# Attention on one Trainium2 core: squares on GpSimd between VectorE passes that read PSUM, two masked evacuations of Q, and more zero matmuls

## The chip, the cores and the metric

The kernel runs on one core of a Trainium2 chip. A core has a matmul engine (TensorE, "PE" in the profile), a vector engine (VectorE, "DVE"), an activation engine (ScalarE, "ACT"), a general engine (GpSimd, "POOL"), which in these kernels works on SBUF alone, and a queue engine (SyncE, "SP"). They run side by side, each takes its own instructions in order, and they wait for each other on semaphores. SBUF and PSUM are the on-chip memories; these kernels use PSUM as eight banks, each for a 128x512 tile of fp32.

The metric is the device time of one execution in microseconds (us), as the median of several runs. Each run also has a mean *granted clock* of TensorE: 1.0 is full speed, 0.5 is half. A run on one core is called slow when it is more than 1.5% above the fastest of the same kernel. Verdicts use the other runs ("fast" ones).

## The reference

Multi-head attention, with batch 1, 2048 positions, width 448 and 16 heads of 28:

```python
qkv = (x @ wqkv).reshape(B, S, 3, H, Dh).transpose(2, 0, 3, 1, 4)
q, k, v = qkv[0], qkv[1], qkv[2]
scores = jnp.einsum("bhqd,bhkd->bhqk", q, k) * (Dh ** -0.5)
p = softmax(scores, axis=-1)
o = jnp.einsum("bhqk,bhkd->bhqd", p, v)
return o.transpose(0, 2, 1, 3).reshape(B, S, D) @ wo
```

There are 16 x 2048 x 2048 exponentials. In tiles of 128 keys by 512 queries that is 1024 tiles, and they set the time of this kernel.

## The kernel before

The work is cut into 16 *windows*: four groups of four heads, times four blocks of 512 queries. A window has 16 rows (128 keys each), and a row has four tiles, one for each head. For each tile TensorE computes scores into PSUM. Another engine turns them into probabilities in SBUF. When all four tiles of a row are there, TensorE adds the row's weighted sum to the output bank `PO`.

Two routes make the probabilities:

- ScalarE takes two tiles at a time (128x1024) with one exponential instruction. It has two double banks, `PA`.
- *Side tiles* go to VectorE. The scores are scaled so that their integer part is the exponent of a bf16 number. The low 16 bits of the fp32 word hold the fraction, and a cubic polynomial of this fraction corrects the mantissa. Three banks, `PD`, serve the side tiles, and also every projection of Q, K, V and the output.

The order of all instructions is made by a small simulation inside the kernel. It walks through time with assumed durations, and decides for each tile which route it takes. On the chip the order is fixed. If an instruction takes longer than assumed, everything behind it on its engine is late. The side route of the kernel before, cut:

```python
def start_pair(tiles, t):                       # two side tiles at once
    for k, (n, sop, slot) in enumerate(tiles):  # pass 1: reads PSUM, writes f16
        p1s.append(add(Op("DVE", 0.6, lambda: nc.vector.tensor_scalar(
            out=DU[b][:, k*QW:(k+1)*QW], in0=lo, scalar1=1.0/65536, scalar2=SS-0.5, ...), ...)))
    q  = add(Op("DVE", ..., nc.vector.tensor_tensor(out=DQ[b], in0=DU[b], in1=DU[b], op=mult)))   # 128x1024
    v  = add(Op("DVE", ..., nc.vector.tensor_scalar(out=DV[b], in0=DU[b], scalar1=C3, scalar2=CE)))
    gq = add(Op("DVE", ..., nc.vector.tensor_tensor(out=DG[b], in0=DQ[b], in1=DV[b], op=mult)))   # 128x1024
    for k, (n, sop, slot) in enumerate(tiles):  # last pass: PSUM plus the cubic
        f = add(Op("DVE", 0.6, nc.vector.scalar_tensor_tensor(out=PTD[..], in0=PD[..], scalar=.., in1=DG[b][..])))
...
if ... d_inflight[0] < ND and backlog(t) < DBACK:      # may one more side tile start?
    ...
    pend_pair.append((n, op, s))
    if len(pend_pair) == 2:                            # only in pairs
        start_pair(list(pend_pair), t); pend_pair.clear()
...
# nothing else to do and little done in the last 3.4 us: one zero matmul,
# but not before the first row of a window
if activity(t) < BAR and ...:
    if pv_next[0] == 0 or j > 0:
        nc.tensor.matmul(out=PO[:], lhsT=zeros[:], rhs=zrow[:], start=first, stop=first, ...)
```

GpSimd does one thing in the steady state: at each window's end it multiplies the copied output by the reciprocal row sums (`OT <- OSB, RRB`, 15 times).

## Time and profile before

| | before |
|---|---|
| median of the first runs | 457.5 us (454.8 to 459.3) |
| span of the profiled run | 450.8 us, mean clock 0.966 |
| ScalarE busy | 417.8 us (93%) |
| VectorE busy | 394.7 us (88%) |
| TensorE busy | 386.6 us (86%) |
| GpSimd busy | 23.0 us (5%) |
| exponential instructions of 128x1024 | 440 |
| side tiles | 144 |
| zero matmuls | 76 |

The page of the kernel before, parts 1 and 2. Part 1 has the busy time and share of each engine. In part 2 each digit is one fortieth of the span, in tenths of busy time. PEclk is the granted clock in tenths.

```profile
span 450.8 us, 7221 instructions
...
PE 386.6 (86%) x2664; PEld 126.2 (28%) x2664; DVE 394.7 (88%) x702; ACT 417.8 (93%) x453; POOL 23.0 (5%) x33
...
PE   7898888889989879789988888879898888888894
...
DVE  4689989889969999999969999999999999489922
ACT  2599999899999999999999999999999999989991
...
PEclk9999999699999998999999999999999989969998
```

ScalarE is at 9 nearly everywhere, and VectorE is close. The clock shows a 6 in two slices. The busy share alone doesn't say what ScalarE loses. For that one looks at the spacing of the exponentials in the timeline. They start 0.905 us apart when nothing is missing. 439 x 0.905 = 397 us, but from the first to the last start it is 416 us. Part of the missing time is seen as waits of the exponentials (line L740) for their scores (waited for: us in total, times; the first exponential of all is 3.4 us of it):

```profile
  PE PA_177 L504: 6.8, 9
  PE PA_178 L504: 4.4, 7
```

Windows of 5 us in the kernel before. The columns are the busy time of PE, weight loads, DVE, ACT and POOL, then granted clock, DMA share and GB/s:

```profile
core 0: us, PE busy (x) PEld busy (x) DVE busy (x) ACT busy (x) POOL busy (x), PEclk, DMA share, GB/s
70.00:75.00 5.00, 4.92 (x36) 1.57 (x36) 4.75 (x9) 5.00 (x7) 0.00 (x0) 1.00 0.00 0
75.00:80.00 5.00, 3.45 (x26) 0.82 (x23) 4.93 (x10) 5.00 (x6) 0.00 (x0) 1.00 0.02 4
80.00:85.00 5.00, 4.42 (x20) 0.94 (x20) 4.93 (x10) 4.37 (x6) 0.00 (x0) 0.69 0.05 8
85.00:90.00 5.00, 4.99 (x23) 0.82 (x22) 3.74 (x6) 3.85 (x4) 1.26 (x1) 0.50 0.13 47
90.00:95.00 5.00, 4.56 (x28) 1.19 (x27) 4.27 (x8) 4.68 (x6) 0.00 (x0) 0.78 0.00 0
```

At 75 to 80 us TensorE is busy for 3.45 of 5 us. Then the clock falls to 0.69 and 0.50, and ScalarE drops from 5.00 to 3.85 us of work.

Timeline of the kernel before around 61 us, VectorE and GpSimd:

```profile
61.36 1.26 POOL L544 TENSOR_TENSOR OT_0_109<-OSB_167,RRB_173 128x512 bf16<-128x512 f32 x1 [57.69 <-DVE DU_159 L562]
...
61.91 1.27 DVE L567 TENSOR_TENSOR DQ_161<-DU_159 128x1024 f16<-128x1024 f16 x1
...
66.79 0.69 DVE L567 TENSOR_TENSOR DQ_162<-DU_160 128x1024 f16<-128x1024 f16 x1
```

The square `DQ_161` lasts 1.27 us while the GpSimd multiply runs, and `DQ_162` 0.69 us without it.

### The profile page before, as it was taken

How to read it: one execution, taken by the hardware profiler on the slowest of the kernel's cores; microseconds unless marked ns; L12 is line 12 of the kernel's file. 1: busy time of each engine (PE TensorE's matmuls, PEld its weight loads, DVE VectorE, ACT ScalarE, POOL GpSimd, SP SyncE). 2: the span in 40 equal slices, each digit the busy share in tenths (PEclk: the TensorE clock that was granted, in tenths of full speed). 3: DMA queues.
4: the chain of work that ended last, by engine and by line, in shares of the span. 5: the costliest groups of instructions: out<-in, count | busy, mean ns of one | idle time of the engine just before them, and what ended most of it. 6: DMA issues, size and time to landing. Idle time of an engine off the chain costs nothing.

```text
span 450.8 us, 7221 instructions
## 1 busy us (share of the span) xinstructions
PE 386.6 (86%) x2664; PEld 126.2 (28%) x2664; DVE 394.7 (88%) x702; ACT 417.8 (93%) x453; POOL 23.0 (5%) x33
## 2 busy tenths in 40 slices
PE   7898888889989879789988888879898888888894
PEld 4522222123322222223322222223332222212232
DVE  4689989889969999999969999999999999489922
ACT  2599999899999999999999999999999999989991
POOL 2000010100100110010100101010101001010000
PEclk9999999699999998999999999999999989969998
DMA  8100000000000010000100000000001000100202
GB/s 267 40 2 0 3 24 0 26 0 4 25 0 15 11 26 0 11 17 2 26 0 25 3 20 6 3 23 2 26 2 25 1 25 3 52 16 0 67 0 84
DMA packets 12364, 9.93 MB, mean 22 GB/s; under 512 B 7208, under 2 KB 9512, under 8 KB 12328
## 3 DMA queue, kind: packets, MB, share of 16 engines
q1 hardware_dynamic: 11112, 9.03, 7.1%
q10 hardware_dynamic: 1216, 0.43, 0.4%
q8 instruction: 21, 0.34, 0.3%
q14 instruction: 15, 0.12, 0.1%
HBM read 7.37 MB, written 1.96 MB: 21 GB/s over the span
## 4 chain that ended last, share of the span: by engine, by line
ACT 50%; DVE 20%; PE 17%; issue 9%; DMA 2%; SPq 0%; ACTq 0%; DVEq 0%
ACT PTA_132 L740 4%; ACT PTA_131 L740 4%; ACT PTA_133 L740 4%; ACT PTA_135 L740 4%; PE PO L666 3%; ACT PTA_144 L740 3%; ACT PTA_134 L740 3%; ACT PTA_137 L740 3%; PE PA_177 L504 3%; PE PA_178 L504 3%; ACT PTA_140 L740 3%; ACT PTA_138 L740 3%; ACT PTA_145 L740 3%; ACT PTA_141 L740 3%; ACT PTA_136 L740 3%
## 5 line engine op out<-in xcount | busy, mean ns | idle before, releaser
L700 PE MATMUL PO<-zrow,zeros 128*128 128x512 bf16 x76 | 29.9, 452 | 1.3 <-DVE zrow L172 1.3
L571 DVE TENSOR_TENSOR DG_165<-DQ_161,DV_163 128x1024 f16<-128x1024 f16 x36 | 26.8, 743 | 1.0
L504 PEld LDWEIGHTS <-KA_92 64*128 64x128 bf16 x256 | 14.4, 94 | 47.1 <-issue 46.4
L567 DVE TENSOR_TENSOR DQ_162<-DU_160 128x1024 f16<-128x1024 f16 x36 | 26.3, 730 | 0.9
L740 ACT ACTIVATE PTA_131<-PA_177 128x1024 bf16<-128x1024 f32 x22 | 23.9, 1086 | 3.4 <-PE PA_177 L504 3.4
L571 DVE TENSOR_TENSOR DG_166<-DQ_162,DV_164 128x1024 f16<-128x1024 f16 x36 | 25.8, 716 | 1.0
L504 PEld LDWEIGHTS <-KA_90 64*128 64x128 bf16 x256 | 14.3, 93 | 43.2 <-issue 41.9
L504 PEld LDWEIGHTS <-KA_89 64*128 64x128 bf16 x256 | 14.1, 94 | 43.4 <-issue 41.6
L567 DVE TENSOR_TENSOR DQ_161<-DU_159 128x1024 f16<-128x1024 f16 x36 | 25.3, 702 | 0.9
L504 PEld LDWEIGHTS <-KA_91 64*128 64x128 bf16 x256 | 13.9, 93 | 40.8 <-issue 39.4
L740 ACT ACTIVATE PTA_137<-PA_177 128x1024 bf16<-128x1024 f32 x21 | 22.1, 1052 | 2.8 <-PE PA_177 L504 2.8
L740 ACT ACTIVATE PTA_140<-PA_178 128x1024 bf16<-128x1024 f32 x22 | 23.5, 1068 | 1.1 <-PE PA_178 L504 1.1
L740 ACT ACTIVATE PTA_138<-PA_178 128x1024 bf16<-128x1024 f32 x20 | 21.5, 1077 | 0.1
L740 ACT ACTIVATE PTA_139<-PA_177 128x1024 bf16<-128x1024 f32 x20 | 21.4, 1068 | 0.0
L740 ACT ACTIVATE PTA_144<-PA_178 128x1024 bf16<-128x1024 f32 x19 | 20.5, 1079 | 0.8 <-PE PA_178 L504 0.8
L740 ACT ACTIVATE PTA_136<-PA_178 128x1024 bf16<-128x1024 f32 x18 | 19.5, 1081 | 1.2 <-PE PA_178 L504 1.2
L740 ACT ACTIVATE PTA_135<-PA_177 128x1024 bf16<-128x1024 f32 x18 | 19.2, 1066 | 0.2 <-PE PA_177 L504 0.2
L562 DVE TENSOR_SCALAR DU_160<-PD_179 128x512 f16<-128x512 uint16 x25 | 17.1, 683 | 2.0 <-PE PD_179 L504 2.0
L740 ACT ACTIVATE PTA_146<-PA_177 128x1024 bf16<-128x1024 f32 x17 | 18.4, 1082 | 0.2 <-PE PA_177 L504 0.2
L740 ACT ACTIVATE PTA_134<-PA_178 128x1024 bf16<-128x1024 f32 x17 | 18.4, 1082 | 0.1
L740 ACT ACTIVATE PTA_142<-PA_178 128x1024 bf16<-128x1024 f32 x17 | 18.3, 1076 | 0.0
L740 ACT ACTIVATE PTA_141<-PA_177 128x1024 bf16<-128x1024 f32 x17 | 18.2, 1070 | 0.1
(606 smaller groups left out, 1324.4 us busy)
## 6 DMA issues: line engine op xcount, KB each, us to landing
RRB_173<-SCR_175 SPq DMA_DIRECT2D x32, 64.0 KB, 2.0
RRB_174<-SCR_176 SPq DMA_DIRECT2D x28, 64.0 KB, 2.0
DCO_169<-OSB_167 SPq DMA_DIRECT2D x32, 2.0 KB, 1.7
XS_125<-in_x_dram SPq DMA_DIRECT2D x1, 448.0 KB
XS_126<-in_x_dram SPq DMA_DIRECT2D x1, 448.0 KB
XS_127<-in_x_dram SPq DMA_DIRECT2D x1, 448.0 KB
XS_128<-in_x_dram SPq DMA_DIRECT2D x1, 448.0 KB, 6.8
DCO_170<-OSB_168 SPq DMA_DIRECT2D x28, 2.0 KB, 1.7
```

The source lines that it names most:

```text
L504: nc.tensor.matmul(out=ap, lhsT=KA[g][r0:r0 + 2 * HP, j * P:(j + 1) * P], rhs=QA[c][i % 2][r0:r0 + 2 * HP, :], start=True, stop=True, tile ...
L562: p1s.append(add(Op("DVE", 0.6, lambda k=k, lo=lo: nc.vector.tensor_scalar(out=DU[b][:, k * QW:(k + 1) * QW], in0=lo, scalar1=1.0 / 65536, ...
L567: q = add(Op("DVE", fx + 0.26 * len(tiles), lambda: nc.vector.tensor_tensor(out=DQ[b][:, 0:w], in0=DU[b][:, 0:w], in1=DU[b][:, 0:w], op=AL ...
L571: gq = add(Op("DVE", fx + 0.26 * len(tiles), lambda: nc.vector.tensor_tensor(out=DG[b][:, 0:w], in0=DQ[b][:, 0:w], in1=DV[b][:, 0:w], op=A ...
L666: nc.tensor.matmul(out=PO[HP * i:HP * (i + 1), :], lhsT=VA[g][:, j, i, :], rhs=r["p"][i][1](), start=(j == 0), stop=(j == NKT - 1), tile_p ...
L700: nc.tensor.matmul(out=PO[:], lhsT=zeros[:], rhs=zrow[:], start=first, stop=first, skip_group_check=True)
L740: nc.scalar.activation(out=PTA[pslot.idx][:, 0:len(ns) * QW], in_=PA[s.idx][:, 0:len(ns) * QW], func=ACT.Exp, bias=ACT_BIAS, scale=ACT_SCALE)
```

## The change

Its intent is to spread the polynomial over two engines, and to keep TensorE's clock up. It has these parts:

1. *Side tiles are started singly* (`start_tile`), each in one of three kinds: the square on GpSimd (kind 2), the whole cubic on GpSimd (kind 0), or all on VectorE in four passes (kind 1). The scheduler picks by GpSimd load and VectorE backlog.
2. *The VectorE passes read the fraction from PSUM each time*, so that no pass of kinds 1 and 2 has two SBUF inputs, and each has PSUM as one input.
3. *Q* is evacuated by two masked passes from PSUM instead of one pass and two short SBUF passes.
4. *The activity bar* for zero matmuls goes from 3600 to 4800.
5. Smaller: six weight paddings go to GpSimd, a chain of projection steps keeps its turn (`CONT`), and there are a few buffers fewer.

The core of the diff (cut; the constants and buffers are left out):

```diff
-BAR = 3600.0
+BAR = 4800.0
...
+    CONT = 1
+    PB0, PB1, DB1, DB2 = 0.5, 2.5, 5.0, 2.0
...
-        ev = add(Op("DVE", 0.66, lambda: nc.vector.tensor_scalar(
-            out=QF[n][:], in0=ap(), scalar1=YSC, scalar2=offscol[:, 0:1], op0=ALU.mult, op1=ALU.add), ...
         for m in range(2):
-            ev = add(Op("DVE", 0.27, lambda m=m: nc.vector.tensor_scalar(
-                out=QA[c][m][:], in0=QF[n][:], scalar1=hmask[m][:, 0:1], scalar2=None, op0=ALU.mult),
+            evs.append(add(Op("DVE", 0.68, lambda m=m: nc.vector.tensor_scalar(
+                out=QA[c][m][:], in0=ap(), scalar1=hmask[m][:, 0:1], scalar2=hoffs[m][:, 0:1],
+                op0=ALU.mult, op1=ALU.add), ...
...
+        elif kind == 2:
+            p1 = add(Op("DVE", 0.6, lambda: nc.vector.tensor_scalar(
+                out=FU[b][:], in0=lo, scalar1=PHK, scalar2=FSC, op0=ALU.add, op1=ALU.mult), ...
+            q = add(Op("POOL", TTP, lambda: nc.gpsimd.tensor_tensor(out=FQ[b][:], in0=FU[b][:], in1=FU[b][:], op=ALU.mult), ...
+            gq = add(Op("DVE", 0.6, lambda: nc.vector.scalar_tensor_tensor(
+                out=FG[b][:], in0=lo, scalar=PHD, in1=FQ[b][:], op0=ALU.add, op1=ALU.mult), ...
...
-                if len(pend_pair) == 2:
-                    start_pair(list(pend_pair), t)
...
+            if pl < PB1 and bl < DB1:
+                kind = 0 if pl < PB0 else 2
+            elif bl < DB2:
+                kind = 1
...
+                start_tile(n, op, s, kind)
```

In the built order this gives 435 exponentials instead of 440, 154 side tiles (119 of kind 2, 21 of kind 0, 14 of kind 1), and 202 zero matmuls.

More of the change, by code (lines that the diff above doesn't have):

```diff
@@ L38 @@
 CK0 = C0 - SS * SS * (C2 - 2 * SS * C3)
+PHK = 65536.0 * (SS - 0.5)
+FSC = math.sqrt(C3 / 65536.0 ** 3)
+PHD = PHK + 65536.0 * CE / C3
 SEM = 0.13
+TTP = 1.27
+TSP = 0.47
 MM = 0.22
@@ L92 @@
     ND = 3
-    NPA = 16
-    NPD = 12
+    NPA = 14
+    CONT = 1
+    PB0, PB1, DB1, DB2 = 0.5, 2.5, 5.0, 2.0
+    NPD = 10
+    NB = 3
     DBACK = 4.0
@@ L116 @@
     QA = [[sb([P, QW], BF16, f"QA{c}_{m}") for m in range(2)] for c in range(NQC)]
-    QF = [sb([P, QW], BF16, f"QF{i}") for i in range(2)]
     KA = [sb([P, S], BF16, f"KA{g}") for g in range(G)]
@@ L127 @@
     PTD = [sb([P, QW], BF16, f"PTD{i}") for i in range(NPD)]
-    DU = [sb([P, 2 * QW], F16, f"DU{i}") for i in range(2)]
-    DQ = [sb([P, 2 * QW], F16, f"DQ{i}") for i in range(2)]
-    DV = [sb([P, 2 * QW], F16, f"DV{i}") for i in range(2)]
-    DG = [sb([P, 2 * QW], F16, f"DG{i}") for i in range(2)]
+    DU = [sb([P, QW], F16, f"DU{i}") for i in range(NB)]
+    DQ = [sb([P, QW], F16, f"DQ{i}") for i in range(NB)]
+    DV = [sb([P, QW], F16, f"DV{i}") for i in range(NB)]
+    DG = [sb([P, QW], F16, f"DG{i}") for i in range(NB)]
+    FU = [sb([P, QW], F32, f"FU{i}") for i in range(NB)]
+    FQ = [sb([P, QW], F32, f"FQ{i}") for i in range(NB)]
+    FG = [sb([P, QW], F32, f"FG{i}") for i in range(NB)]
+    EU = [sb([P, QW], F32, f"EU{i}") for i in range(2)]
+    EQ = [sb([P, QW], F32, f"EQ{i}") for i in range(2)]
+    EG = [sb([P, QW], F32, f"EG{i}") for i in range(2)]
     OSB = [sb([P, QW], F32, f"OSB{i}") for i in range(2)]
@@ L148 @@
     onescol = sb([P, 1], F32, "onescol")
-    offscol = sb([P, 1], F32, "offscol")
     hmask = [sb([P, 1], F32, f"hmask{m}") for m in range(2)]
+    hoffs = [sb([P, 1], F32, f"hoffs{m}") for m in range(2)]
     tc_order = ctx.enter_context(tc.manual_schedule())
@@ L192 @@
         for i in (m, m + 2):
-            nc.vector.memset(hmask[m][HP * i:HP * (i + 1), :], 1.0)
-    nc.vector.tensor_scalar(out=offscol[:], in0=onescol[:], scalar1=YTOP, scalar2=None, op0=ALU.mult)
+            nc.vector.memset(hmask[m][HP * i:HP * (i + 1), :], YSC)
+        nc.vector.tensor_scalar(out=hoffs[m][:], in0=onescol[:], scalar1=hmask[m][:, 0:1], scalar2=YTOP / YSC,
+                                op0=ALU.mult, op1=ALU.mult)
     for g in range(G):
@@ L294 @@
         for (W, WP, nm, win) in ((WK, WKP, "k", wkin), (WQ, WQP, "q", wqin)):
-            eng = "DVE"
-            w_ready[(nm, g)] = add(Op(eng, 0.3, pad_w(W, WP, g, eng), deps=[win if g == 0 else wrest],
-                                      prio=-1005 + (nm == "q") if g == 0 else g * 256 - 230 - 1000,
-                                      elig=None if g == 0 else lead(g * 256 - 230, 20)))
+            eng = "DVE" if g == 0 else "POOL"
+            w_ready[(nm, g)] = add(Op(eng, 0.3 if g == 0 else 0.6, pad_w(W, WP, g, eng), deps=[win if g == 0 else wrest],
+                                      prio=-1005 + (nm == "q") if g == 0 else -900 + g))
     kev = {}
@@ L392, in task_Q @@
                     deps=[ab, nkop[g]], prio=prio - (1000 if w else 0), lat=PLAT, kind="B"))
-        ev = add(Op("DVE", 0.66, lambda: nc.vector.tensor_scalar(
-            out=QF[n][:], in0=ap(), scalar1=YSC, scalar2=offscol[:, 0:1], op0=ALU.mult, op1=ALU.add),
-            deps=[bd], prio=prio - (1000 if w else 0), elig=elig))
+        evs = []
+        for m in range(2):
+            evs.append(add(Op("DVE", 0.68, lambda m=m: nc.vector.tensor_scalar(
+                out=QA[c][m][:], in0=ap(), scalar1=hmask[m][:, 0:1], scalar2=hoffs[m][:, 0:1],
+                op0=ALU.mult, op1=ALU.add), deps=[bd] + evs, prio=prio - (1000 if w else 0), elig=elig)))
+        ev = evs[-1]
         ev.after = lambda t: setattr(task["slot"], "free_at", t + SEM)
-        for m in range(2):
-            ev = add(Op("DVE", 0.27, lambda m=m: nc.vector.tensor_scalar(
-                out=QA[c][m][:], in0=QF[n][:], scalar1=hmask[m][:, 0:1], scalar2=None, op0=ALU.mult),
-                deps=[ev], prio=prio - (1000 if w else 0), elig=elig))
         qev[(g, c)] = ev
@@ L488 @@
     acts = []
-    pend_pair = []
     pv_next = [0]
@@ L509, in s_ready @@
         return qev[(g, c)].done(t) and kev[(g, j // TPC)].done(t)
-    fin_state = {}
     last_evac = []
@@ L551 @@
     d_inflight = [0]
-    def start_pair(tiles, t):
-        b = fin_state.setdefault("db", 0) % 2
-        fin_state["db"] += 1
-        prevl = fin_state.get(("last", b))
-        w = len(tiles) * QW
-        p1s = []
-        for k, (n, sop, slot) in enumerate(tiles):
-            lo = PD[slot.idx][:].bitcast(U16).rearrange("p (n two) -> p n two", two=2)[:, :, 0]
-            p1s.append(add(Op("DVE", 0.6, lambda k=k, lo=lo: nc.vector.tensor_scalar(
-                out=DU[b][:, k * QW:(k + 1) * QW], in0=lo, scalar1=1.0 / 65536, scalar2=SS - 0.5,
-                op0=ALU.mult, op1=ALU.add), deps=[sop] + ([prevl] if prevl else []), prio=n)))
-        n0 = tiles[0][0]
-        fx = 0.065
-        q = add(Op("DVE", fx + 0.26 * len(tiles), lambda: nc.vector.tensor_tensor(
-            out=DQ[b][:, 0:w], in0=DU[b][:, 0:w], in1=DU[b][:, 0:w], op=ALU.mult), deps=p1s, prio=n0 - 1))
-        v = add(Op("DVE", fx + 0.135 * len(tiles), lambda: nc.vector.tensor_scalar(
-            out=DV[b][:, 0:w], in0=DU[b][:, 0:w], scalar1=C3, scalar2=CE, op0=ALU.mult, op1=ALU.add), deps=p1s, prio=n0 - 1))
-        gq = add(Op("DVE", fx + 0.26 * len(tiles), lambda: nc.vector.tensor_tensor(
-            out=DG[b][:, 0:w], in0=DQ[b][:, 0:w], in1=DV[b][:, 0:w], op=ALU.mult), deps=[q, v], prio=n0 - 1))
-        for k, (n, sop, slot) in enumerate(tiles):
-            w_, g, c, j, i = tile_of(n)
-            ps = fin_state.setdefault("ptd", 0)
-            st = {"s": None}
-            def acq(t, st=st):
-                if st["s"] is None:
-                    free = [s for s in ptd_slots if s.free_at <= t + 1e-9]
-                    if not free:
-                        return False
-                    st["s"] = min(free, key=lambda s: s.free_at)
-                    st["s"].free_at = 1e18
-                return True
-            def fin(st=st, k=k, slot=slot):
-                nc.vector.scalar_tensor_tensor(out=PTD[st["s"].idx][:].bitcast(U16), in0=PD[slot.idx][:],
-                                               scalar=EBITS + CK0, in1=DG[b][:, k * QW:(k + 1) * QW], op0=ALU.add, op1=ALU.add)
-            f = add(Op("DVE", 0.6, fin, deps=[gq], prio=n0 - 2, acq=acq))
-            def aft(t, slot=slot, n=n, st=st):
-                slot.free_at = t + SEM + 0.2
-                d_inflight[0] -= 1
-            f.after = aft
-            rows.setdefault((w_, j), {"p": {}})["p"][i] = (f, lambda st=st: PTD[st["s"].idx][:], ("d", st))
-            fin_state[("last", b)] = f
@@ new lines, with start_tile, acq, aft @@
+    d_buf = [[0] * 3]
+    d_last = {}
+    def start_tile(n, sop, slot, kind):
+        nb = 2 if kind == 1 else NB
+        b = d_buf[0][kind] % nb
+        d_buf[0][kind] += 1
+        prev = d_last.get((kind, b))
+        w_, g, c, j, i = tile_of(n)
+        lo = PD[slot.idx][:].bitcast(U16).rearrange("p (n two) -> p n two", two=2)[:, :, 0]
+        if kind == 0:
+            p1 = add(Op("DVE", 0.6, lambda: nc.vector.tensor_scalar(
+                out=DU[b][:], in0=lo, scalar1=1.0 / 65536, scalar2=SS - 0.5, op0=ALU.mult, op1=ALU.add),
+                deps=[sop] + ([prev] if prev else []), prio=n - 20))
+            q = add(Op("POOL", TTP, lambda: nc.gpsimd.tensor_tensor(out=DQ[b][:], in0=DU[b][:], in1=DU[b][:], op=ALU.mult),
+                       deps=[p1], prio=n, lat=0.2))
+            v = add(Op("POOL", TSP, lambda: nc.gpsimd.tensor_scalar(
+                out=DV[b][:], in0=DU[b][:], scalar1=C3, scalar2=CE, op0=ALU.mult, op1=ALU.add),
+                deps=[p1], prio=n - 0.5, lat=0.2))
+            gq = add(Op("POOL", TTP, lambda: nc.gpsimd.tensor_tensor(out=DG[b][:], in0=DQ[b][:], in1=DV[b][:], op=ALU.mult),
+                        deps=[q, v], prio=n, lat=0.3))
+            src = DG[b]
+        elif kind == 2:
+            p1 = add(Op("DVE", 0.6, lambda: nc.vector.tensor_scalar(
+                out=FU[b][:], in0=lo, scalar1=PHK, scalar2=FSC, op0=ALU.add, op1=ALU.mult),
+                deps=[sop] + ([prev] if prev else []), prio=n - 20))
+            q = add(Op("POOL", TTP, lambda: nc.gpsimd.tensor_tensor(out=FQ[b][:], in0=FU[b][:], in1=FU[b][:], op=ALU.mult),
+                       deps=[p1], prio=n, lat=0.25))
+            gq = add(Op("DVE", 0.6, lambda: nc.vector.scalar_tensor_tensor(
+                out=FG[b][:], in0=lo, scalar=PHD, in1=FQ[b][:], op0=ALU.add, op1=ALU.mult), deps=[q], prio=n - 25))
+            src = FG[b]
+        else:
+            p1 = add(Op("DVE", 0.6, lambda: nc.vector.tensor_scalar(
+                out=EU[b][:], in0=lo, scalar1=PHK, scalar2=C3 / 65536.0 ** 3, op0=ALU.add, op1=ALU.mult),
+                deps=[sop] + ([prev] if prev else []), prio=n))
+            q = add(Op("DVE", 0.6, lambda: nc.vector.scalar_tensor_tensor(
+                out=EQ[b][:], in0=lo, scalar=PHK, in1=EU[b][:], op0=ALU.add, op1=ALU.mult), deps=[p1], prio=n - 1))
+            gq = add(Op("DVE", 0.6, lambda: nc.vector.scalar_tensor_tensor(
+                out=EG[b][:], in0=lo, scalar=PHD, in1=EQ[b][:], op0=ALU.add, op1=ALU.mult), deps=[q], prio=n - 1))
+            src = EG[b]
+        st = {"s": None}
+        def acq(t):
+            if st["s"] is None:
+                free = [s for s in ptd_slots if s.free_at <= t + 1e-9]
+                if not free:
+                    return False
+                st["s"] = min(free, key=lambda s: s.free_at)
+                st["s"].free_at = 1e18
+            return True
+        f = add(Op("DVE", 0.61, lambda: nc.vector.scalar_tensor_tensor(
+            out=PTD[st["s"].idx][:].bitcast(U16), in0=PD[slot.idx][:], scalar=EBITS + CK0, in1=src[:],
+            op0=ALU.add, op1=ALU.add), deps=[gq], prio=n - 30, acq=acq))
+        def aft(t):
+            slot.free_at = t + SEM + 0.2
+            d_inflight[0] -= 1
+        f.after = aft
+        rows.setdefault((w_, j), {"p": {}})["p"][i] = (f, lambda: PTD[st["s"].idx][:], ("d", st))
+        d_last[(kind, b)] = f
@@ L621, in try_pe @@
                 return op
-        if USE_D and pos[0] < NT - 24 and s_ready(pos[0], t) and d_inflight[0] < ND and backlog(t) < DBACK:
-            free = [s for s in d_slots if s.free_at <= t + 1e-9]
-            if free:
-                s = min(free, key=lambda s: s.free_at)
+        if USE_D and pos[0] < NT - 24 and s_ready(pos[0], t) and d_inflight[0] < ND:
+            free_d = [s for s in d_slots if s.free_at <= t + 1e-9]
+            bl = backlog(t)
+            kind = None
+            pl = pool_load(t)
+            if pl < PB1 and bl < DB1:
+                kind = 0 if pl < PB0 else 2
+            elif bl < DB2:
+                kind = 1
+            if free_d and kind is not None:
+                s = min(free_d, key=lambda s: s.free_at)
                 s.free_at = 1e18
@@ L631, in try_pe @@
                 op = Op("PE", MM, lambda n=n, s=s: emit_S(n, PD[s.idx][:]), lat=PLAT, kind="D")
-                pend_pair.append((n, op, s))
-                if len(pend_pair) == 2:
-                    start_pair(list(pend_pair), t)
-                    pend_pair.clear()
-                return op
-        if pend_pair and pos[0] >= NT - 24:
-            start_pair(list(pend_pair), t)
-            pend_pair.clear()
+                start_tile(n, op, s, kind)
+                kinds[kind] += 1
+                return op
         pv = None
@@ L656, in try_pe @@
                     break
-        if pv is not None and (st is None or pv_turn[0] or pos[0] - pv_next[0] * HG > 40):
+        if pv is not None and (st is None or (pv_turn[0] and not (CONT and st.acq is None)) or pos[0] - pv_next[0] * HG > 40):
             w, g, c, j, r = pv
@@ L714, with pool_load @@
     last_fam = [None]
+    kinds = [0, 0, 0]
     def backlog(t):
-        return (sum(o.dur for o in static["DVE"] if o.elig is None or o.elig(t)) + max(0.0, free["DVE"] - t)
-                + (1.0 if pend_pair else 0.0))
+        return sum(o.dur for o in static["DVE"] if o.elig is None or o.elig(t)) + max(0.0, free["DVE"] - t)
+    def pool_load(t):
+        return sum(o.dur for o in static["POOL"] if o.prio > -500) + max(0.0, free["POOL"] - t)
     act_i = [0]
@@ L820 @@
                 heapq.heappush(times, t + 0.15)
-    assert pv_next[0] == NROW and act_i[0] == len(acts) and not pend_pair, (pv_next, NROW, act_i, len(acts), pos)
+    assert pv_next[0] == NROW and act_i[0] == len(acts), (pv_next, NROW, act_i, len(acts), pos)
     assert not any(static[e] for e in static), {e: len(static[e]) for e in static}
```

## The prediction

> **What bounds it now.** ScalarE. The built instruction order has 440 exponentials of 128x1024; in the timeline their start-to-start time is 0.905 us when nothing is missing. 439 x 0.905 = 397 us, but the first starts at 21.8 us and the last at 438.0: about 18 us are lost between exponentials. The rest is head (22) and tail (13). By windows of 50 us ScalarE is mostly 97 to 100% busy, VectorE 90 to 98%, TensorE 81 to 91%.
>
> The 18 us, by the timeline:
> - about 9 us where the granted TensorE clock falls to 0.5 to 0.7 (55-60, 80-95, 168-175, 365-370, 395-403 us; mean clock 0.966). Each fall follows some 3 us with TensorE only 40 to 70% busy, mostly where a 512-query window has ended and the next one's first row waits for a VectorE tile. The Trainium skill (TensorE: Matmul & The Clock Gate, Part 1) says that an idle activity window of about 3.4 us halves the clock; this trace agrees in kind.
> - about 9 us of short stalls (0.3 to 1.0 us): TensorE, in order, waits for VectorE to free a PSUM bank or deliver a tile (251, 274, 326 us), and ScalarE starves. VectorE is late in part because passes with two SBUF inputs last up to 1.6 us instead of 0.69 while GpSimd multiplies. The skill (SBUF — State Buffer, "Who interferes with whom") describes this as an exclusive shared port.
>
> **What the change does.**
> - Exponentials 440 to 435: 5 x 0.905 = 4.5 us off the critical engine. 154 instead of 144 tiles go elsewhere: 119 with the square on GpSimd, 21 with the cubic there, 14 all on VectorE.
> - VectorE per such tile: before 4.26 us per pair = 2.13. After: three passes at 0.60 = 1.8; two 1.2; four dependent ones, estimated from 0.60 to 0.72 each, 2.7. Sum 307 to about 279 us; Q evacuation 19.4 to 21.1; six weight pads leave. VectorE gains about 27 us of slack.
> - No new VectorE tile pass reads two SBUF tensors, so the port conflict should vanish, although GpSimd runs 161 more multiplies at about 1.27 us (undisturbed time of today's) plus 21 short ops: 23 to about 240 us busy, no bottleneck. Today's normalising multiply starts 10 to 11.4 us after its evacuation, so it should rarely hold up GpSimd's queue.
> - Zero matmuls 76 to 202: about +28 us of TensorE time in idle slots. They should prevent some clock falls, not all: they stay forbidden before a window's first row, where most falls begin. They leave TensorE less room: about 0.3 us lies between a freed bank and ScalarE needing it.
>
> **Sum.** 4.5 (fewer exponentials) + about 4 (half the clock loss) + about 3 (a third of the stalls) - about 1 (new stalls from the VectorE-GpSimd-VectorE chain and zero matmuls) = 10.5 us. 457.5 - 10.5 = 447.
>
> Predicted 447 us, range 439 to 456. Faster by over 2%: 0.52; within 2%: 0.43; slower: 0.05.
>
> **What would show each step.** ScalarE: 435 exponentials still 0.905 apart; first-to-last about 405 us instead of 416. Clock: mean 0.98 or more, fewer falls. VectorE: about 370 us busy instead of 395, no tile pass over 1 us. GpSimd: about 240 us busy, multiplies near 1.27 us. Fewer TensorE waits on VectorE.
>
> **What would make it wrong.** Squares much longer than 1.3 us, or held up by VectorE, so that TensorE waits for tiles and ScalarE starves; zero matmuls standing in front of score matmuls; clock falls that stay because window ends are not filled (then about 451); or a clock that never falls (then about 441).

## More of the kernel before

The timeline of the kernel before around 383 us (start, duration, engine, line, operation, output<-input; in brackets how long the engine had been idle and who ended it). These are one side tile's score matmul, its first VectorE pass, its last one, and the weighted sum that needed it. Its partner's score matmul stands between them:

```profile
382.96 0.37 PE L504 MATMUL PD_180<-QA_0_83,KA_92 64*128 64x512 bf16 x1
...
393.06 0.37 PE L504 MATMUL PD_181<-QA_1_84,KA_92 64*128 64x512 bf16 x1
393.35 0.68 DVE L562 TENSOR_SCALAR DU_160<-PD_180 128x512 f16<-128x512 uint16 x1
...
396.85 0.69 DVE L588 SCALAR_TENSOR_TENSOR PTD_147<-PD_180,DG_166 128x512 uint16<-128x512 f32 x1
...
397.98 0.61 PE L666 MATMUL PO<-PTD_147,VA_108 128*32 128x512 bf16 x1
```

The tile in bank `PD_180` had its scores at 383.0 us, but VectorE touched it first at 393.35 us, because a pair starts only when its second tile exists. That one (`PD_181`) came at 393.06 us. The row had to wait, and it was the first row of a window, before which no zero matmul is allowed.

```profile
L569 DVE TENSOR_SCALAR DV_163<-DU_159 x36: 364/419/1501, 28.8 to 422.4; 128x1024 f16<-128x1024 f16 x36
```

By the trace, the seven `DV` passes that overlap a GpSimd multiply take 0.88 us in the mean, and the other 65 take 0.42.

## The result, and the profile after

The changed kernel took 436.6 us (median; 436.4 to 437.5). The kernel before took 458.4 us (454.8 to 460.0). The ratio is 0.954, with a 95% interval from 0.948 to 0.960. A ratio here is the mean time of one kernel's fast runs over that of the other's of the same rounds, so it isn't quite the ratio of the medians. The time lies below the predicted range: the gain is about 21 us where 10.5 were predicted.

The page after, the same parts as above:

```profile
span 434.9 us, 7592 instructions
...
PE 396.0 (91%) x2755; PEld 133.0 (31%) x2790; DVE 373.5 (86%) x632; ACT 409.5 (94%) x448; POOL 206.3 (47%) x221
...
PE   7899999999999989899999999898998999899994
...
DVE  4589898998999999998889999999999898987822
ACT  2589999999999999999999999999999999999991
...
PEclk9999999999999999999999999999999999999999
```

The clock is at 9 in every slice, and the mean is 0.998. The 5 us windows of the changed kernel at the same place of the run:

```profile
70.00:75.00 5.00, 4.80 (x31) 1.45 (x30) 4.53 (x8) 5.00 (x7) 1.77 (x3) 1.00 0.01 3
75.00:80.00 5.00, 4.49 (x30) 1.30 (x29) 3.79 (x7) 5.00 (x6) 3.56 (x4) 1.00 0.01 0
80.00:85.00 5.00, 4.80 (x35) 1.53 (x34) 5.00 (x10) 5.00 (x7) 1.30 (x2) 1.00 0.03 3
85.00:90.00 5.00, 4.49 (x33) 1.30 (x32) 4.93 (x9) 5.00 (x6) 2.86 (x3) 1.00 0.21 52
90.00:95.00 5.00, 4.80 (x29) 1.46 (x25) 4.77 (x9) 5.00 (x7) 2.28 (x3) 1.00 0.00 0
```

ScalarE now works 5.00 of 5 us throughout. From the first exponential to the last it is 398.8 us instead of 416.2. The waits of ScalarE in the changed kernel (engine, output, line, waited for: us in total, times, longest) hold one wait of an exponential, which is the first one of all:

```profile
ACT XT_63 L289 <- DVE XT_63 L287: 6.7, 1, 6.7
ACT XS_126 L888 <- PE PA_190 L886: 4.6, 1, 4.6
ACT PTA_129 L772 <- PE PA_190 L515: 3.8, 1, 3.8
ACT KA_87 L354 <- DVE KPART_91 L351: 2.1, 2, 1.1
ACT L179 <- PEq L907: 1.7, 1, 1.7
ACT OSB_180 L865 <- DVE OSB_180 L864: 1.0, 1, 1.0
ACT XS_126 L888 <- PE PA_191 L886: 0.6, 1, 0.6
ACT VA_103 L438 <- PE PD_194 L425: 0.4, 1, 0.4
```

The new passes in the changed kernel. For one buffer each: the VectorE pass that multiplies by the square, and GpSimd's square (minimum/median/maximum in ns, first and last start, shapes):

```profile
L592 DVE SCALAR_TENSOR_TENSOR FG_173<-PD_192,FQ_170 x17: 630/681/693, 38.0 to 406.2; 128x512 f32<-128x512 uint16 x17
```

```profile
L590 POOL TENSOR_TENSOR FQ_168<-FU_165 x40: 1037/1041/1043, 33.2 to 407.6; 128x512 f32<-128x512 f32 x40
```

No such VectorE pass is longer than 0.693 us, and no square is longer than 1.045 us.

### The profile page after: what moved, and what is told of

It is laid out like the page before. It is cut to its first block, busy times and chain, and to the rows that moved or that the text cites. A ratio compares the mean times of both kernels' runs of the same rounds, so it can differ in the third digit from the quotient of the medians.

```text
span 434.9 us, 7592 instructions
## 1 busy us (share of the span) xinstructions
PE 396.0 (91%) x2755; PEld 133.0 (31%) x2790; DVE 373.5 (86%) x632; ACT 409.5 (94%) x448; POOL 206.3 (47%) x221
## 2 busy tenths in 40 slices
DMA packets 12366, 9.95 MB, mean 23 GB/s; under 512 B 7208, under 2 KB 9512, under 8 KB 12328
## 4 chain that ended last, share of the span: by engine, by line
ACT 65%; PE 19%; issue 10%; DVE 3%; DMA 2%; another core or an unknown queue 0%; ACTq 0%; DVEq 0%
ACT PTA_129 L772 6%; ACT PTA_131 L772 6%; ACT PTA_133 L772 6%; ACT PTA_134 L772 5%; ACT PTA_130 L772 5%; ACT PTA_132 L772 5%; ACT PTA_135 L772 5%; ACT PTA_137 L772 5%; ACT PTA_138 L772 4%; ACT PTA_136 L772 4%; ACT PTA_142 L772 4%; ACT PTA_139 L772 4%; ACT PTA_141 L772 3%; PE PA_190 L515 3%; ACT PTA_140 L772 3%
## 5 line engine op out<-in xcount | busy, mean ns | idle before, releaser
L590 POOL TENSOR_TENSOR FQ_168<-FU_165 128x512 f32<-128x512 f32 x40 | 41.6, 1041 | 50.4 <-DVE FU_165 L587 50.1
L590 POOL TENSOR_TENSOR FQ_170<-FU_167 128x512 f32<-128x512 f32 x39 | 40.6, 1041 | 49.2 <-DVE FU_167 L587 49.2
L728 PE MATMUL PO<-zrow,zeros 128*128 128x512 bf16 x170 | 60.9, 403 | 3.2 <-issue 1.9
L590 POOL TENSOR_TENSOR FQ_169<-FU_166 128x512 f32<-128x512 f32 x40 | 41.6, 1040 | 38.3 <-DVE FU_166 L587 38.0
L728 PEld LDWEIGHTS <-zeros 128*128 128x128 bf16 x202 | 16.9, 99 | 43.0 <-issue 41.5
L772 ACT ACTIVATE PTA_135<-PA_190 128x1024 bf16<-128x1024 f32 x24 | 26.9, 1121 | 0.0
L515 PEld LDWEIGHTS <-KA_90 64*128 64x128 bf16 x256 | 14.4, 93 | 40.7 <-issue 40.2
L515 PEld LDWEIGHTS <-KA_88 64*128 64x128 bf16 x256 | 15.0, 93 | 38.3 <-issue 36.2
L772 ACT ACTIVATE PTA_134<-PA_191 128x1024 bf16<-128x1024 f32 x24 | 26.6, 1109 | 0.0
L515 PEld LDWEIGHTS <-KA_87 64*128 64x128 bf16 x256 | 15.2, 93 | 36.1 <-issue 34.8
L772 ACT ACTIVATE PTA_136<-PA_191 128x1024 bf16<-128x1024 f32 x23 | 26.0, 1129 | 0.0
L515 PEld LDWEIGHTS <-KA_89 64*128 64x128 bf16 x256 | 14.8, 93 | 35.1 <-issue 33.3
L772 ACT ACTIVATE PTA_133<-PA_190 128x1024 bf16<-128x1024 f32 x21 | 24.1, 1148 | 0.0
L772 ACT ACTIVATE PTA_137<-PA_190 128x1024 bf16<-128x1024 f32 x20 | 22.7, 1134 | 0.0
L772 ACT ACTIVATE PTA_141<-PA_190 128x1024 bf16<-128x1024 f32 x20 | 22.3, 1115 | 0.0
L772 ACT ACTIVATE PTA_129<-PA_190 128x1024 bf16<-128x1024 f32 x17 | 18.6, 1093 | 3.8 <-PE PA_190 L515 3.8
L772 ACT ACTIVATE PTA_138<-PA_191 128x1024 bf16<-128x1024 f32 x19 | 21.5, 1132 | 0.0
L772 ACT ACTIVATE PTA_132<-PA_191 128x1024 bf16<-128x1024 f32 x19 | 21.3, 1123 | 0.0
L772 ACT ACTIVATE PTA_142<-PA_191 128x1024 bf16<-128x1024 f32 x18 | 20.4, 1134 | 0.0
L772 ACT ACTIVATE PTA_131<-PA_190 128x1024 bf16<-128x1024 f32 x18 | 20.1, 1115 | 0.0
L772 ACT ACTIVATE PTA_139<-PA_190 128x1024 bf16<-128x1024 f32 x18 | 19.9, 1108 | 0.0
L772 ACT ACTIVATE PTA_130<-PA_191 128x1024 bf16<-128x1024 f32 x17 | 18.9, 1112 | 0.0
```

The costliest lines, as they stand in the source:

```text
L515: nc.tensor.matmul(out=ap, lhsT=KA[g][r0:r0 + 2 * HP, j * P:(j + 1) * P], rhs=QA[c][i % 2][r0:r0 + 2 * HP, :], start=True, stop=True, tile ...
L590: q = add(Op("POOL", TTP, lambda: nc.gpsimd.tensor_tensor(out=FQ[b][:], in0=FU[b][:], in1=FU[b][:], op=ALU.mult), deps=[p1], prio=n, lat=0 ...
L772: nc.scalar.activation(out=PTA[pslot.idx][:, 0:len(ns) * QW], in_=PA[s.idx][:, 0:len(ns) * QW], func=ACT.Exp, bias=ACT_BIAS, scale=ACT_SCALE)
```

## The experiments

All outputs are right. "Clock" is the mean granted clock of the fast runs. In these traces the buffer numbers are left out of the names. Runs of one group shared a chip, and each time was taken beside runs of the kernel before.

For reading the results I made a yardstick from two measured numbers. The first is the spacing of 0.905 us for each exponential. The second is the clock: the kernel before ran 28 times beside the experiments, and 4 times as one of them, on three chips, from 452.1 us (clock 0.970) to 464.3 us (clock 0.929). A straight line through these 32 points has a slope of 2.92 us for each 0.01 of clock, and misses the points by 0.8 us (root mean square). The kernel is the same in all 32. I take the waits it has apart from the clock as the same too; that is not shown, and a wait that brings a fall would count in the slope. Without the three slow points the slope is 2.75. The changed kernel with and without zero matmuls (a_same and a_fill0 below) gives 2.80 for each 0.01. So the yardstick, an estimate that goes on with the line above the clocks it was drawn from, is

  time = 436.2 + 0.905 x (exponentials - 435) + 2.92 x (0.997 - clock) / 0.01 + rest

where 436.2 us and 0.997 are the mean of the changed kernel when it was run again (a_same below). The rest is what neither term explains: stalls.

| run | exponentials | zero matmuls | median us of fast runs | clock | exponentials' term | clock's term | rest |
|---|---|---|---|---|---|---|---|
| b_same (before) | 440 | 76 | 456.5 | 0.951 | 4.5 | 13.4 | 3.1 |
| b_fill | 440 | 175 | 449.7 | 0.981 | 4.5 | 4.6 | 4.4 |
| b_normdve | 441 | 86 | 447.5 | 0.981 | 5.4 | 4.7 | 1.3 |
| b_single | 437 | 91 | 446.7 | 0.995 | 1.8 | 0.7 | 8.4 |
| b_db3 | 446 | 120 | 463.4 | 0.980 | 10.0 | 5.0 | 12.3 |
| b_all | 439 | 208 | 440.7 | 0.994 | 3.6 | 0.9 | 0.3 |
| a_same (changed) | 435 | 202 | 436.0 | 0.997 | 0.0 | -0.1 | 0.1 |
| a_ref (changed) | 435 | 202 | 436.0 | 0.998 | 0.0 | -0.2 | 0.2 |
| a_fill3600 | 435 | 92 | 438.1 | 0.995 | 0.0 | 0.5 | 1.2 |
| a_fill0 | 435 | 0 | 452.4 | 0.938 | 0.0 | 17.2 | -0.6 |
| a_dveonly4 | 446 | 219 | 446.9 | 0.994 | 10.0 | 0.9 | -0.2 |
| a_cont0 | 438 | 204 | 440.4 | 0.998 | 2.7 | -0.2 | 1.7 |
| a_pair3600 | 439 | 98 | 442.1 | 0.993 | 3.6 | 1.2 | 0.5 |
| a_lock | 436 | 188 | 442.6 | 0.986 | 0.9 | 3.1 | 1.8 |
| a_td3 | 428 | 256 | 464.9 | 0.984 | -6.3 | 3.9 | 31.1 |
| a_best | 432 | 189 | 434.1 | 0.996 | -2.7 | 0.4 | 0.6 |

The rests are worked out from means of fast runs, and good to about 1 us; with the slope of 2.75 they rise by up to 0.8 us (a_fill0: 1.0). Edits change the built order too, so runs differ in more than the edited lines: their numbers of exponentials and zero matmuls are in the table. Labels with b_ start from the kernel before, those with a_ from the changed one.

### First group: is it the zero matmuls or the relief of VectorE?

**b_same**: the kernel before, again, for the clock of its runs.

> The kernel before, unchanged, to get the granted clock of every run. Its traced run took 452.7 us, the median of its runs 458.4. If clock falls explain the spread, the slower runs have the lower mean clock: about 0.966 near 452.7 us and about 0.94 to 0.95 near 459. If they do not, the clock is about the same in all runs and the spread has another cause.

It took 456.5 us. The spread of the kernel before is the clock: its fastest run here has 0.973 and its slowest 0.943. The traced run that the prediction was read from (452.7 us, clock 0.966) had lost less than the usual run.

**b_fill**: only the bar.

```diff
-BAR = 3600.0
+BAR = 4800.0
```

> The kernel before with only the higher activity bar (4800 instead of 3600): 175 zero matmuls instead of 76, still 440 exponentials, VectorE work unchanged. Theory C (clock): the zero matmuls alone remove nearly all clock falls and with them about 15 us: clock 0.99 or more, 442 to 446 us, but the short waits of TensorE on VectorE remain. Theory R (relief of VectorE): the falls come from late VectorE tiles at window ends, where zero matmuls are forbidden, so they stay: clock 0.96 to 0.98, 451 to 457 us.

It took 449.7 us at clock 0.981, a ratio of 0.987 (0.981 to 0.993). Neither theory is met in full. The time is 1.3 us under theory R's range and 3.7 above theory C's. More zero matmuls take away about two thirds of the clock loss, and nothing of the stalls (rest 4.4 against 3.1).

**a_fill3600**: the changed kernel with the old bar.

```diff
-BAR = 4800.0
+BAR = 3600.0
```

> The changed kernel with the old activity bar (3600): 92 zero matmuls instead of 202, 435 exponentials, the VectorE/GpSimd split kept. Theory C: the clock falls come back, mean clock 0.95 to 0.975, 446 to 452 us. Theory R: the split alone keeps TensorE fed, clock 0.985 or more, 437 to 441 us.

It took 438.1 us at clock 0.995, as theory R had it. With the new side route, the higher bar is worth about 2 us (roughly, since a_same ran on another chip).

**a_fill0**: the changed kernel without zero matmuls.

```diff
-BAR = 4800.0
+BAR = 0.0
```

> The changed kernel without any zero matmul (none at the start either), 435 exponentials. Theory C: many clock falls, mean clock below 0.95, over 452 us. Theory R: little lost after the start, 438 to 445 us.

Its fast runs took 452.4 us at clock 0.938 (453.5 with the slow one), as theory C had it, and the rest is -0.6: by the yardstick all of the loss is clock. In its trace the first fall comes at 166 us, so it is not the missing matmuls at the start. So zero matmuls as such are needed. The new route needs few of them (92 are enough), and the old route isn't cured by many (175).

How long does TensorE stand at the end of a window? From the timelines I took the gap from the end of a window's last weighted sum to the start of the next window's first, for the 15 window ends. In the traced run of the kernel before the five longest are 12.1, 4.1, 3.9, 3.8 and 3.5 us, and the longest of the changed kernel is 2.4. I also took the share of time in which any matmul record runs, in every stretch of 3.4 us. In the kernel before the lows are 0.47 (at 50 us), 0.40 (77), 0.50 (155), 0.51 (166), 0.51 (182), 0.44 (361) and 0.51 (392). The clock falls come at 55, 82, 171, 365 and 396 us, each 4 to 6 us after the start of such a low; the lows at 155 and 182 brought none. In the changed kernel no stretch lies below 0.62, and there is no fall before the end of the work.

Why did the lows at 155 and 182 us bring none? In each of the 18 traces all changes of the clock lie on a grid of 3.413 us (to within 1 ns); where the grid begins differs from trace to trace. So the share can be taken anew in the stretches of this grid, at full clock, from 25 us on until 14 us before the end. Of 17 stretches with a share under 0.58, 16 ended in a fall; of 82 between 0.58 and 0.70, 16; of 1981 above 0.70, none. The lows at 155 and 182 us lie across two or more stretches of the grid, of which none is below 0.69. The lowest stretch of the changed kernel is 0.71. (Some matmul records are missing in some traces, so a share can be a little too low.)

### Second group: which part of the new side route?

Three things differ in the route: tiles go singly, VectorE passes no longer have the form that GpSimd holds up, and VectorE has less to do.

**b_single**: the kernel before with single tiles.

```diff
-                if len(pend_pair) == 2:
+                if len(pend_pair) == 1:
```

> The kernel before, with each side tile started alone instead of in pairs; still five f16 passes on VectorE, no GpSimd, old activity bar: 437 exponentials, 91 zero matmuls, 150 side tiles. Theory P (the pair delays the first tile of a pair, so the first row of a window comes late and the window gap passes 3 us): window gaps below 3 us, clock 0.99 or more, 439 to 444 us. Theory S (VectorE lacks slack; only moving work to GpSimd cures it): VectorE stays over 90% busy, its lateness stays, clock 0.95 to 0.975, 449 to 456 us.

It took 446.7 us at clock 0.995. The clock is as theory P has it, and the time is not (439 to 444). The falls are nearly gone, but a rest of 8.4 us has come: VectorE is full (410.1 us busy), and TensorE waits for its tiles. The waits of b_single, of a weighted sum for a side tile:

```profile
PE PO L666 <- DVE PTD L588: 7.4, 17, 1.4
```

Of the 14 such waits over 0.2 us, seven (4.4 of 6.9 us, with the longest) end within 5 us of the start of a VectorE pass that GpSimd had held up; for the others no such pass is near.

**b_db3**: pairs kept, fewer side tiles.

```diff
-    DBACK = 4.0
+    DBACK = 3.0
```

> The kernel before with fewer side tiles (backlog limit 3.0 instead of 4.0): still pairs, 446 exponentials, 120 zero matmuls, 134 side tiles, so about 285 us of VectorE tile work, as in the changed kernel. Theory S: with that slack the falls vanish; six more exponentials cost 5.4 us, so clock 0.99 or more and 445 to 450 us. Theory P: the pairs still delay the first row, gaps over 3 us stay, clock 0.96 to 0.98, 454 to 460 us.

It took 463.4 us at clock 0.980 (ratio 1.022, 1.017 to 1.027), slower than both theories allow. Giving VectorE slack by letting it take fewer tiles made half pairs wait. Window gaps of 9.95, 5.1, 4.9 and 4.7 us appeared. This is one of them in the timeline of b_db3, first the score matmul of half a pair, then the first pass on it, then the weighted sum:

```profile
227.18 0.38 PE L504 MATMUL PD<-QA,KA 64*128 64x512 bf16 x1
...
233.56 0.68 DVE L562 TENSOR_SCALAR DU<-PD 128x512 f16<-128x512 uint16 x1
...
239.19 0.61 PE L666 MATMUL PO<-PTD,VA 128*32 128x512 bf16 x1
```

The half pair stood from 227.2 to 233.6 us. So this run speaks for theory P, but it did not test theory S cleanly.

**b_normdve**: the normalising multiply on VectorE, so that GpSimd is idle.

```diff
-        o5 = add(Op("POOL", 1.3, lambda: nc.gpsimd.tensor_tensor(out=OT[g][c][:], ...
+        o5 = add(Op("DVE", 0.68, lambda: nc.vector.tensor_tensor(out=OT[g][c][:], ...
```

> The kernel before with the 15 normalising multiplies moved from GpSimd to VectorE, so that GpSimd can hold up no VectorE pass: 441 exponentials, 86 zero matmuls. Theory L (shared-port lock is the source of the lateness): passes over 1 us vanish, the short stalls and most falls go, clock 0.98 or more, 446 to 451 us. Theories P and S: within 1% of before, clock about 0.955.

It took 447.5 us at clock 0.981, a ratio of 0.987 (0.982 to 0.992): theory L's time, and its clock. The same pass in the kernel before and in b_normdve (minimum/median/maximum in ns):

```profile
L571 DVE TENSOR_TENSOR DG_165<-DQ_161,DV_163 x36: 679/692/1641, 29.8 to 422.9; 128x1024 f16<-128x1024 f16 x36
```

```profile
L571 DVE TENSOR_TENSOR DG<-DQ,DV x71: 678/692/693, 31.0 to 426.3; 128x1024 f16<-128x1024 f16 x71
```

The hold-ups are gone (maximum 693 instead of 1641 ns), and the rest has gone from 3.1 to 1.3 us. So fifteen GpSimd multiplies of about 1.3 us each cost the kernel before, by the yardstick, some 2 us of stalls and part of its clock falls. That part is not isolated: the built order has 86 zero matmuls instead of 76. Its trace still has a window gap of 9.6 us: half a pair, with its score at 124.1 us, stood until 132.3, as its partner came at 131.8, and the clock fell at 137.6. So a waiting half pair brings a fall without any hold-up by GpSimd.

**a_dveonly4**: the changed kernel without GpSimd in its tiles.

```diff
-            if pl < PB1 and bl < DB1:
+            if False:
...
-    PB0, PB1, DB1, DB2 = 0.5, 2.5, 5.0, 2.0
+    PB0, PB1, DB1, DB2 = 0.5, 2.5, 5.0, 4.0
```

> The changed kernel with GpSimd taken out of the tiles (all 133 side tiles of the four-pass form on VectorE, backlog limit 4): 446 exponentials, 219 zero matmuls. Theory P: gaps short because tiles go singly; clock 0.99 or more; eleven more exponentials than the changed kernel cost 10 us: 445 to 449 us. Theory S: VectorE full again (about 350 us of tile work), clock 0.98 or less and stalls: 450 to 458 us.

It took 446.9 us at clock 0.994: theory P's number. The rest is -0.2 although VectorE is 92% busy. In this kernel GpSimd's part is just the eleven exponentials that it spares ScalarE (10.0 us by count, 10.6 measured in means against a_same, which ran on another chip).

### Third group: small edits against the whole change

**a_same**: the changed kernel as the yardstick of this group.

> The changed kernel, unchanged, on the same chip as the three runs beside it: 435 exponentials, clock 0.995 or more, 436 to 438 us.

It took 436.0 us.

**b_all**: the kernel before with three small edits, and no GpSimd in the tiles at all.

```diff
-                if len(pend_pair) == 2:
+                if len(pend_pair) == 1:
...
-        o5 = add(Op("POOL", 1.3, lambda: nc.gpsimd.tensor_tensor(out=OT[g][c][:], ...
+        o5 = add(Op("DVE", 0.68, lambda: nc.vector.tensor_tensor(out=OT[g][c][:], ...
...
-BAR = 3600.0
+BAR = 4800.0
```

> The kernel before with three small edits and no GpSimd in the tiles: side tiles started singly, the normalising multiply on VectorE (no shared-port hold-ups), activity bar 4800. 439 exponentials, 208 zero matmuls, VectorE about 410 us busy. Theory P+L (only half pairs, hold-ups and clock falls cost time): 439 to 441 us, that is the changed kernel plus four exponentials (3.6 us). Theory S (a full VectorE keeps being late): TensorE still waits 5 us or more for VectorE tiles, 443 to 448 us.

It took 440.7 us at clock 0.994, as theory P+L had it: 4.7 us above a_same, of which four exponentials are 3.6. The ratio to the kernel before is 0.965 (0.959 to 0.971). So about 16 of the 21 us can be had without GpSimd. VectorE is nearly as full as in b_single (401.9 us busy, 92% in both), and yet such waits are down from 7.4 to 1.1 us. So being full isn't the fault by itself. That being held up in an unplanned way is the fault fits half of the waits in b_single; but b_all also has the higher bar, and no run tells the two apart. The square in b_single and in b_all:

```profile
L567 DVE TENSOR_TENSOR DQ<-DU x150: 353/412/1483, 27.0 to 420.6; 128x512 f16<-128x512 f16 x150
```

```profile
L567 DVE TENSOR_TENSOR DQ<-DU x146: 362/423/448, 26.2 to 414.8; 128x512 f16<-128x512 f16 x146
```

**a_cont0**: the old turn rule.

```diff
-    CONT = 1
+    CONT = 0
```

> The changed kernel with the old turn rule between weighted sums and the steps of a projection chain: 438 exponentials, 204 zero matmuls. If the rule matters only through the three exponentials that the schedule then gives to ScalarE: 439 to 440 us, clock 0.995. If it also keeps the clock or TensorE's order: above 441 us or clock below 0.99.

It took 440.4 us at clock 0.998. Three exponentials are 2.7 us, and 1.7 are left over. The expectation (439 to 440) was missed by 0.4 us. In this run the window gaps go up to 5.9 us with no fall of the clock: TensorE had projections to do in most of them, and its lowest 3.4 us stretches are 0.51 (once) and otherwise above 0.62. On the grid of the clock its lowest stretch is 0.68. A long gap is thus not enough for a fall.

**a_td3**: looser limits, so that still fewer tiles go to ScalarE.

```diff
-TTP = 1.27
-TSP = 0.47
+TTP = 1.06
+TSP = 0.62
...
-    PB0, PB1, DB1, DB2 = 0.5, 2.5, 5.0, 2.0
+    PB0, PB1, DB1, DB2 = 0.5, 4.0, 7.0, 3.0
```

> The changed kernel with GpSimd durations as measured (1.06 us for a multiply, 0.62 for the short op) in its scheduler and looser limits (GpSimd load 4.0, VectorE backlog 7.0 and 3.0): 428 exponentials, 256 zero matmuls, 168 side tiles. If ScalarE's count is still the whole cost: 7 x 0.905 = 6.3 us less, 430 to 432 us. If side tiles now come late (no VectorE-only tiles, longer queues): window gaps over 3 us, stalls, 434 to 442 us.

It took 464.9 us, the slowest of all, though it has the fewest exponentials (428). The waits of a_td3, and one of them in its timeline:

```profile
ACT PTA L772 <- PE PA L515: 30.0, 11, 7.5
```

```profile
303.37 1.53 DVE L408 TENSOR_SCALAR QA<-PD,hmask,hoffs 128x512 bf16<-128x512 f32 x2
...
304.73 1.94 ACT L772 ACTIVATE PTA<-PA 128x1024 bf16<-128x1024 f32 x2 [3.42 <-PE PA L515]
...
304.95 0.39 PE L515 MATMUL PA<-QA,KA 64*128 64x512 bf16 x2 [0.33 <-DVE QA L408]
```

ScalarE has stood still for 3.42 us. Its next scores need the Q of the new window, and VectorE had evacuated it only then (303.37 us). Side tiles and projections share three banks and VectorE. That the side tiles pushed the projections back is read from this place only; I have not tested it apart.

### Fourth group: the parts put back, and a faster version

**a_ref**: the changed kernel on the chip of this group.

> The changed kernel, unchanged, as the yardstick of this chip: 435.5 to 438 us, clock 0.995 or more.

It took 436.0 us.

**a_pair3600**: the changed kernel, holding side tiles until there are two, with the old bar.

```diff
-                start_tile(n, op, s, kind)
...
+                held.append((n, op, s, kind))
+                if len(held) == 2:
+                    for a in held:
+                        start_tile(*a)
+                    held.clear()
...
+        if held and pos[0] >= NT - 24:                 # and the same at the end
...
-BAR = 4800.0
+BAR = 3600.0
```

> The changed kernel with the old activity bar (98 zero matmuls) and with side tiles held until a second one is issued, as in the kernel before; 439 exponentials. Its twin without holding took 438.1 us at clock 0.995 with 435 exponentials. If holding is what brings the clock falls: window gaps over 3 us, clock 0.985 or less, 446 us or more. If it only costs its four exponentials: 441 to 443 us, clock 0.99 or more.

It took 442.1 us at clock 0.993. Holding cost its four exponentials, and little more. The falls did not come back, and the longest window gap was 3.2 us. So pairs alone do not make the falls. In the kernel before they stood beside a full and held-up VectorE. The hold-ups are not needed (b_normdve); whether the full VectorE is, is not shown.

**a_lock**: one pass with two SBUF inputs back on VectorE, for the 26 tiles of kind 0.

```diff
-            gq = add(Op("POOL", TTP, lambda: nc.gpsimd.tensor_tensor(out=DG[b][:], in0=DQ[b][:], in1=DV[b][:], op=ALU.mult),
-                        deps=[q, v], prio=n, lat=0.3))
+            gq = add(Op("DVE", 0.35, lambda: nc.vector.tensor_tensor(out=DG[b][:], in0=DQ[b][:], in1=DV[b][:], op=ALU.mult),
+                        deps=[q, v], prio=n - 25))
```

> The changed kernel with the last multiply of the 26 cubic tiles moved from GpSimd to VectorE as a pass with two f16 SBUF inputs; 436 exponentials. If GpSimd's squares hold such passes up: these 26 passes last up to 1.4 us instead of about 0.43, or the squares beside them last over 1.1 us; 437 to 441 us. If there is no conflict in this setting: all near 0.43 us and 436.5 to 437.5 us.

Its fast runs took 442.6 us; the runs spread from 439.0 us (clock 0.998) to 446.2 (0.973, a slow one), and the table has the fast ones. The time is above the range. The pass in question (minimum/median/maximum in ns):

```profile
L583 DVE TENSOR_TENSOR DG<-DQ,DV x26: 408/602/1287, 28.3 to 408.1; 128x512 f16<-128x512 f16 x26
```

A pass of this shape takes about 0.43 us undisturbed (b_all: median 423 ns), and here half of them take over 0.6 and the longest 1.29 us. The 18 that overlap a GpSimd instruction take 0.91 us in the mean, the other eight 0.42. Only 26 of them brought clock falls back in three of four runs, with a window gap of 7.3 us in the traced one. So the form of the VectorE passes, one PSUM input and at most one SBUF input, is what lets GpSimd run beside them.

**a_best**: measured GpSimd durations in the scheduler, and slightly moved limits.

```diff
-TTP = 1.27
-TSP = 0.47
+TTP = 1.06
+TSP = 0.62
...
-    PB0, PB1, DB1, DB2 = 0.5, 2.5, 5.0, 2.0
+    PB0, PB1, DB1, DB2 = 0.8, 2.5, 5.5, 2.0
```

> The changed kernel with the measured GpSimd durations in its scheduler (1.06 and 0.62 us) and slightly moved limits (0.8, 2.5, 5.5, 2.0): 432 exponentials, 189 zero matmuls, 160 side tiles. Count alone: 3 x 0.905 = 2.7 us less than a_ref, 433 to 434 us. If the tighter plan has no room for the chip's deviations: 436 us or more.

It took 434.1 us (433.5 to 436.1) against 436.0 (435.3 to 437.4) of a_ref on the same chip: 1.9 us less by medians, 1.7 by means, where three exponentials are 2.7. It is the fastest version here, but three rounds aren't enough to be sure of so small a step.

## Why the prediction was wrong

Where the 20 us went, by the yardstick: the 32 runs of the kernel before have a mean of 456.3 us at clock 0.956. 456.3 - 436.2 = 20.1 us. The exponentials are 4.5, the clock is (0.997 - 0.956) x 292 = 12.0, and the rest, 3.6, is stalls. With the fast runs alone (slope 2.75) the same sum gives 10.8 for the clock and 4.2 for stalls, out of 19.5.

- *"4.5 (fewer exponentials)"* was right: 435 were run, still about 0.90 us apart (median).
- *"about 4 (half the clock loss)"* is the step that failed. The runs show 11 to 12, which is all of it. Two things went wrong in it. The loss was sized at 9 us from a trace that was one of the better runs (clock 0.966; the mean is 0.956), when the line through the runs gives 12 for the usual one. And the falls were expected to stay at the window ends, because zero matmuls are still forbidden there. They went away: the gaps at the window ends shortened, from 12.1 us at most to 2.4. (The prediction's last line had a clock that never falls, at about 441. It came, and the larger loss, no new stalls and somewhat more saved stalls make up the rest to 436.6.) From the score matmul to the finished tile, one in ten side tiles took over 8.6 us before and the slowest 14.6; after, one in ten took over about 6.3 (kind 2) and the slowest of all 8.7. The medians hardly differ (5.7 and 5.3). The prediction had costed the new tiles by their mean work, and had not asked what their worst delay was or what half a pair waits for, although the wait of 10 us at 383 us was in the trace. That earlier tiles are what shortened the gaps is read from these traces and from the runs of the second group; no run isolates it.
- *"about 3 (a third of the stalls)"* was near: 3.6 by the yardstick. But in the traced runs the waits of exponentials on TensorE vanished, all but the first one.
- *"about 1 (new stalls ...)"* did not come. VectorE waited 2 us in all for squares.
- The port conflict was right in kind, and it was under-valued: removing it alone (b_normdve) took about 6 us off. The Trainium skill (SBUF — State Buffer, "Who interferes with whom") states that a VectorE instruction with two SBUF inputs contends with a GpSimd instruction that reads SBUF. The traces agree: 1.64 us instead of 0.69 before, no such pass over 0.69 us without GpSimd (b_normdve), and again up to 1.29 us in a_lock. The prediction looked at passes with two SBUF inputs alone; `DV`, with one, was held up as well (1.50 us instead of 0.42 before, at most 0.42 in b_normdve).
- GpSimd: 206 us busy, not 240, because a square of one tensor takes 1.04 us, not the 1.27 of a product of two. VectorE: 373.5 us busy, where about 370 were predicted; the masked evacuations of Q took 0.80 us each, 25.3 in all instead of 21.1.
- Zero matmuls did not get in the way of score matmuls: with 202 of them only the first exponential waited for TensorE, and with 92 (a_fill3600) the kernel was no faster.

Which part brought how much does not add up to one number for each, since the clock loss can be saved only once. From the kernel before, the bar alone, single tiles alone, and freeing the passes from GpSimd alone give about 6 us each (ratios of 0.986 to 0.987). All three give 16. The move of the squares to GpSimd adds the last 4 to 5 us, mostly through fewer exponentials. The evacuation of Q, the weight paddings and the buffers were not tested apart; b_all does without them. What stays open is how much each of a full VectorE and of hold-ups adds to the falls in the kernel before: a_pair3600 shows only that pairs by themselves don't suffice, and no run gave the kernel before slack without touching its pairs.

## What to carry to other kernels

- In a statically ordered kernel, look at the slowest tenth of a side path and not at its mean work: an item that waits for a partner, or a pass that another engine can hold up, stops TensorE in order, and the clock fall afterwards can cost more than the stall (here 11 to 12 us against about 4).
- Plot a few runs' time against their granted clock before costing a change. Here one line gave the clock's share (2.8 to 2.9 us for each 0.01), and showed that the single traced run understated it.
- If GpSimd is to work beside VectorE, give VectorE passes one input from PSUM and at most one from SBUF. Then the GpSimd work of 140 tiles disturbed no pass; it did with 26 passes of two SBUF inputs, and in the kernel before also with a pass of a single SBUF input (`DV`).

## What the Trainium skill lacked or had wrong

- *TensorE: Matmul & The Clock Gate*, Part 1, tells of an idle window that halves the clock. No section of the page gives a busy share at which this happens. In these traces TensorE was not idle: of the grid stretches of 3.413 us in which matmul records covered under 0.58 of the time, 16 of 17 ended in a fall to 0.5; between 0.58 and 0.70 it was 16 of 82, and above 0.70 none of 1981. Lows of 0.50 that lay across two stretches brought no fall, which fits the page's free-running window.
- The same page does not say whether matmuls of zeros hold the clock up. They do: with the same 435 exponentials, the clock was 0.938 with none, 0.995 with 92 and 0.997 with 202 of them.
- *GPSIMD Engine Reference*, section 3.1, gives one rate for two-input elementwise work, taken from an fp32 add. A square of one fp32 128x512 tensor took 1.04 us, a product of two fp32 tensors (bf16 output) 1.27, and of two f16 tensors 1.16.
- The same page's table of engine selection (section 4.1) calls one-input work on GpSimd "roughly line-rate". The one-input pass of 512 f16 elements took 0.62 us on GpSimd, and 0.28 us on VectorE (`DV` in b_single, median), so beside VectorE it was 2.2 times as long.
